# Sliding-window attention gated by a SwiGLU block: prologue, output stores, and weight casts tied to the last exponential

## The chip, the cores and the metric

The kernel runs on one core of a Trainium2 chip. A core has a tensor engine (PE, with its weight loads shown apart as PEld), a vector engine (DVE), a scalar engine (ACT), GpSimd (POOL) and a sync engine (SP), which here issues nearly all DMAs. Each engine works through its own list of instructions in order and waits on semaphores. The metric is the device time of one execution in microseconds (us); lower is better.

## The reference

The input x has 2048 tokens of 512 features. It is normalised once (layer norm without weights), and two branches read the result:

```
xn = layernorm(x)
q, k, v = split(xn @ wqkv)                 # 32 heads of 16
p = softmax(mask(q k^T / 4))               # each token sees itself and the 255 before it
s = (p v) @ wo                             # 512 -> 512
g = silu( (silu(xn @ w1) * (xn @ w3)) @ w2 )   # 512 -> 1792 -> 512
out = x + s * g
```

All inputs and the output are float32.

## The kernel before, in words

**Precision.** PE multiplies float16. A float32 operand is scaled by a power of two and cut into a high part (its float16 cast) and a low part (the rest, again float16); three products stand for one. The scale of a weight block comes from the sum of its squares. So each weight block has a path of its own: a load, squares (L249 on ACT or L251 on DVE for w1, w3 and the projections, L923 on ACT for w2), a cast of the sums (L261), a small matmul that adds them over the partitions (L285 when it stands beside scores), a chain of small DVE operations (L294 to L304, then L886 and L887, or L935 to L945 for w2), and the cut. `split_pool` makes the cut of most blocks: ACT scales (L342) and casts (L343), POOL subtracts in four pieces (L345). `split` does the same with ACT (L333) and DVE (L334).

**Tiles.** Tokens go in four tiles of 512 (t = 0 to 3). The hidden width of 1792 is 14 blocks f of 128. For each tile and block, `gate_up` makes 24 matmuls of 128x512 (L1036) into two PSUM banks; ACT takes a tanh (L1051) from one, DVE multiplies (L1055, L1060). `down` (L1261) multiplies by w2 in four groups of blocks: 0 to 3, 4 to 7, 8 to 10 and 11 to 13. In tile 0 the weights are prepared and stored to device memory; later tiles load them ready made. Tiles 2 and 3 use a folded product with w2 (L1179).

**Attention.** 32 units of four heads each (t, g, p): four head groups g and two pairs p in a tile. `pass1` makes scores (L665) and DVE takes their maxima (L679); a later pass, `pass2`, makes scores again transposed (L746), DVE adds the mask (L753), ACT takes the exponential (L756), and PE multiplies by the values (L774). `project` makes keys and queries (L597), whose banks ACT (L614) and DVE (L618) empty; they go to device memory and `fetch` (L641) brings them back in another layout. `total` multiplies by wo (L1313), joins the branches and stores the output (L1324).

**PSUM.** Two single banks `m0` and `m1` are taken in turn by `bank()`; two pairs of banks `s` hold scores (`scores_bank()`); one pair `po` holds the result of attention and some scores.

**What sets the order.** The Python program traces instructions one after another. PE's order is exactly the traced one. On the other engines a scheduler sets the order at build time: among instructions that are ready in its own model of time it takes those traced first, with a priority for what is traced inside `urgent()` (exponentials, tanh, and what empties banks among them). It can therefore put an instruction ahead of others that were traced before it. `tc.issue_after(ins)` forbids that for one instruction: what is traced in it comes behind `ins` on `ins`'s engine. `behind_exp()` is this with the last exponential traced so far; before the change it was used for the squares of w2 (L923) and a few more.

**Steps.** Time in the program is counted in steps: one after each batch of attention rows and after each piece of dense work (six matmuls, mostly). `later(n, f)` runs f when n more steps have passed. `beside_scores(n, f)` puts f, after n steps, at the head of the list from which a batch of `pass1` takes its next side work. `measure(f, apart)` does the squares of blocks f and f + 1 (both w1 and w3), `apart` steps from each other, then the scale beside scores after 8 steps, then the four cuts: 1, 2, 4 and 6 steps behind the scale for f below 8, else 1, 5, 9 and 13. `measure_down(k, f)` does it for group k of w2, with the cuts 1, 3, 5 and 7 steps behind.

**The prologue** (L1505 to L1596) loads x and the first weights while PE runs filler matmuls (`keep_busy`, L1537). It normalises and transposes tile 0 and projects head groups 0 and 1, with `fetch` one step behind each. The scores of the first unit begin at the first L665.

SBUF for weights and streams is a list of 54 slots, `take` and `give`; a slot that is given back can name a number of steps before it is taken again.

Of the kernel before, what the change touches and what calls it, by code (L numbers as in the profile page):

```python
# [10 lines left out]
F32 = mybir.dt.float32  # L11
# [10 lines left out]
P = 128  # L22
S = 2048
D = 512
# [59 lines left out]
def tile_block(ctx: ExitStack, tc: tile.TileContext, x, wqkv, wo, w1, w3, w2, out):  # L84
# [155 lines left out]
    def squares(parts, on_act=0, apart=0):  # L240


        ssq = small.tile([P, len(parts)], F32, name="ssq")

        def one(i, raw):

            sq = ppool.tile([P, D], BF16, name="sqa" if i < on_act else "junk", bufs=1)
            if i < on_act:
                nc.scalar.activation(sq, raw, AF.Square, accum_out=ssq[:, i:i + 1])  # L249
# [12 lines left out]
        def behind_bank():  # L262

            with tc.issue_after(lasts["emptied"].ins) if "emptied" in lasts else nullcontext():
                cast()
        if apart:
            later(apart * (len(parts) + 1) + 1, behind_bank)
        else:
            cast()
        return sb  # L270
# [310 lines left out]
    def project(t, g, k, terms=(range(3),), scores_bank=False):  # L581
# [7 lines left out]
        def part(n):  # L589
# [1 line left out]
            w = WQ[t, g, k]  # L591
            xh, xl = X[t]
            if n == 0:
                cell["pp"] = pss.tile([P, 2, TW], F32, name="s")[:, 0, :] if scores_bank else bank([P, TW])
            for c, i in parts[n]:
                a, b = ((0, xh), (1, xh), (0, xl))[i]
                nc.tensor.matmul(cell["pp"], w[:, (a * NC + c) * P:(a * NC + c + 1) * P], b[:, c, :], start=(c, i) == parts[0][0],  # L597
# [33 lines left out]
        WQ[t, g, k] = w = take(F16)  # L631
        nc.sync.dma_start(w, dWQ[g, k])

    def fetch(t, g):
        QA[t, g] = qa = qpool.tile([P, 4, TW], F16, name="qa")
        ka = keys(t, g)
        c0 = 0 if t else 2 * P
        for dst, d in ((ka[:, :, c0:], dK[g][:, :, t * TW - 2 * P + c0:(t + 1) * TW]),
                       (qa, dQ[g][:, :, t * TW:(t + 1) * TW])):
            for r in range(2):  # L640
                lasts["load"] = nc.sync.dma_start(dst[64 * r:64 * r + KR],  # L641
                                  d[64 * r:64 * r + 64].rearrange("(a d) i t -> (d i) a t", d=DH))

# [224 lines left out]

    measured = set()

    def measure(f, apart=0):

        raws = [RAW.pop(f + i) for i in range(2)]
        sb = squares([raws[0][0], raws[1][0], raws[0][1], raws[1][1]], on_act=4 if f > 2 else 2, apart=apart)
# [7 lines left out]
        def rest(pp, pi):  # L884
            ff = slice(f, f + 2)
            nc.vector.tensor_scalar(sg_scale[:, ff], pp[:, 0, :], 0.5 / (WS * XS), None, op0=ALU.mult)  # L886
            nc.vector.tensor_mul(p13[:, ff], pp[:, 0, :], pp[:, 1, :])  # L887
            measured.update((f, f + 1))

            def cut(i, k):  # L890
                if k == 0:
                    WF[0, f + i] = [[None, None], WF.pop((0, f + i), [None, None])[1]]
                WF[0, f + i][0][k] = a = take(F16)
                split_pool(a[:, 0:D], a[:, D:], raws[i][k], pi[:, k, i:i + 1])
                give(raws[i][k], after=5)
            for i in range(2):
                for k in range(2):
                    later(((1, 2, 4, 6) if f < 8 else (1, 5, 9, 13))[2 * i + k], lambda i=i, k=k: cut(i, k))
        if started:
            beside_scores(8, scale)  # L900
        else:
            later(10 if apart else 6, scale)

# [11 lines left out]
    def measure_down(k, f):  # L915
# [17 lines left out]
        def rest(p2):  # L933
# [13 lines left out]
            def cut(f):  # L947
                raw = RAW2.pop(f)
                WF.setdefault((0, f), [[None, None], None])[1] = b = take(F16)
                if k == 0:  # L950
                    with tc.issue_after(lasts["emptied"].ins):
                        split(b[:, 0:D], b[:, D:], raw, sw[:, f - f0:f - f0 + 1])
                else:
                    split_pool(b[:, 0:D], b[:, D:], raw, sw[:, f - f0:f - f0 + 1])
                give(raw, after=5)
            for i, f in enumerate(range(f0, f1)):
                later(1 + 2 * i, lambda f=f: cut(f))
# [335 lines left out]
    def total(t, b):  # L1293
# [4 lines left out]
        def part(half):  # L1298
# [16 lines left out]
            if half:  # L1315
# [10 lines left out]
                if t == NT - 1:  # L1326
                    store()
                else:
                    later(4, store)
                if b == 3:  # L1330
                    give(*(OT[t, g] for g in range(NG)))
        return opening([(6, lambda h=h: part(h)) for h in range(2)])
# [22 lines left out]
    def feed_forward():  # L1355
# [4 lines left out]
        for t in range(NT):  # L1360
            for f in range(FB):
                if t == 0:
# [3 lines left out]
                    elif f + LEAD == FB - 1:  # L1366
                        pieces += [(0, lambda f=f: load(0, f)) for f in range(FB - 2, FB)]
                    if f % 2 and f + 3 < FB:
                        pieces.append((0, lambda f=f + 3: later(5, lambda: measure(f, 1)) if f == 6 else measure(f, 1)))
# [161 lines left out]
        nc.gpsimd.memset(KA[2][:, a, :].bitcast(F32), TWO_ONES)  # L1531


    def keep_busy(n):
        ps = bank([P, 4, P])
        for _ in range(n):
            nc.tensor.matmul(ps, onesb, onesb.unsqueeze(1).to_broadcast([P, 4, P]), start=True, stop=True)  # L1537

# [19 lines left out]
        flush()  # L1558
    with tc.issue_after(lasts["hi"].ins), tc.issue_after(lasts["x"].ins):
        qk[1][1]()  # L1560
    keep_busy(4)


    k00, q00 = (project(0, 0, k, ((0,), (1,), (2,)), k) for k in (1, 0))
    run([k00[0], q00[0], k00[1]])
    qk[1][2]()
    with tc.issue_after(lasts["scale"].ins):
# [2 lines left out]
    qk[1][3]()  # L1570
    with tc.issue_after(lasts["hi"].ins):
        run([k00[2], q00[2]])
    later(1, lambda: fetch(0, 0))
    k01 = project(0, 1, 1, ((0, 2), (1,)))
    run(k01[:1])
    wv[2]()
# [4 lines left out]
    sc["o"] = scaled(SQ["wv"][3], OS / WS, "so")  # L1581
    with tc.issue_after(lasts["hi"].ins):
        measure(0)
    run(project(0, 1, 0, scores_bank=True))
    later(1, lambda: fetch(0, 1))
    run(value(0, True))
    qk[2][1]()
# [89 lines left out]
```

## Time and profile before

| | |
|---|---|
| runs, median (lowest to highest) | 811.51 us (811.1 to 811.94), 3 runs |
| the profiled execution | 811.24 us |
| its span, from the first to the last instruction | 809.4 us |
| PE busy | 793.7 us of the span |
| DVE busy | 631.2 us |
| ACT busy | 392.1 us |
| POOL busy | 377.1 us |
| granted clock of PE | 1.00 in all stretches |

All durations below come from the profiled execution, whose own time is 811.24 us. A row of the timeline gives the start and the duration in us, the engine, the line, the operation, what it writes and reads, the count of instructions that the row joins, and in brackets the idle time of that engine before it and what ended it. A row of the waits gives who waited for whom, the sum, the times and the longest. A row of the stretches gives the stretch, its length, the busy time of PE, PEld, DVE, ACT and POOL with their counts, the granted clock, the busy share of the DMA engines and GB/s. An "SPq" row is a DMA issue on SP's queue, not the transfer.

### The profile page before, as it was taken

The numbers are of one execution on the slowest core, as the hardware profiler recorded it, in microseconds if no ns is written. First come the engines' busy times: TensorE is split into PE (matmuls) and PEld (weight loads), VectorE is DVE, ScalarE is ACT, GpSimd is POOL, SyncE is SP. The second block draws the span as 40 slices with busy tenths as digits, with TensorE's granted clock in tenths as the row PEclk, the third lists the DMA queues.
The fourth block names the chain that finished last, engine by engine and source line by source line (L and its number), as shares of the span: only waits on it lengthen the run. The fifth ranks groups of instructions, "written<-read, shape, count | busy, mean of one in ns | idle before, by whom it ended". The sixth has DMA issues, their size and how long they took to land.

```text
span 809.4 us, 23944 instructions
## 1 busy us (share of the span) xinstructions
PE 793.7 (98%) x9176; PEld 403.7 (50%) x9176; DVE 631.2 (78%) x2037; ACT 392.1 (48%) x591; POOL 377.1 (47%) x732
## 2 busy tenths in 40 slices
PE   8999989999999999999999999999999999999998
PEld 4444444444444444444444454456544754466465
DVE  8788788887888777887988888777778787875437
ACT  6879586553546544345344433344444234344411
POOL 2345376342329445354353455530346276550670
PEclk9999999999999999999999999999999999999999
DMA  9968554835576474757655634646372644335321
GB/s 282 265 214 267 160 183 134 278 114 191 160 199 208 134 232 139 218 142 263 160 162 181 194 104 119 185 137 179 105 201 74 160 139 137 113 90 172 111 65 62
DMA packets 109795, 134.19 MB, mean 166 GB/s; under 512 B 18864, under 2 KB 64880, under 8 KB 109680
## 3 DMA queue, kind: packets, MB, share of 16 engines
q1 hardware_dynamic: 109392, 132.13, 54.6%
q8 instruction: 72, 1.18, 0.6%
q10 hardware_dynamic: 288, 0.52, 0.2%
q14 instruction: 43, 0.35, 0.1%
HBM read 91.23 MB, written 36.57 MB: 158 GB/s over the span
## 4 chain that ended last, share of the span: by engine, by line
PE 79%; DVE 8%; ACT 6%; DMA 3%; issue 2%; SPq 1%; POOL 0%; ACTq 0%; DVEq 0%
PE m L1036 30%; PE po L774 8%; PE m L1261 8%; PE m L1179 8%; PE m L597 7%; PE s L746 5%; PE m L1313 4%; PE m L567 4%; PE s L665 3%; DMA slot<-in_B_w_dram 2%; DVE junk L679 2%; PE po L665 2%; ACT slot L342 1%; ACT pt L756 1%; ACT sqa L249 1%
## 5 line engine op out<-in xcount | busy, mean ns | idle before, releaser
L1036 PE MATMUL m<-XH,slot 128*128 128x512 f16 x896 | 267.4, 380 | 1.6 <-DVE slot L618 1.2
L756 ACT ACTIVATE pt<-s,es 128x1024 f32<-128x1024 f32 x152 | 167.5, 1112 | 193.7 <-DVE s L753 186.5
L1036 PEld LDWEIGHTS <-slot 128*128 128x128 f16 x1344 | 124.7, 98 | 156.0 <-issue 12.0
L1036 PE MATMUL m<-XL,slot 128*128 128x512 f16 x448 | 169.9, 379 | 0.0
L753 DVE TENSOR_TENSOR s<-s,MK 128x256 f32<-128x256 f32 (+2 forms) x280 | 118.7, 434 | 51.2 <-PE s L746 47.0
L679 DVE CUSTOM_DVE_ANT_0 junk<-s,MW 128x320 bf16<-128x320 f32 x276 | 133.9, 485 | 17.9 <-PE s L665 10.3
L339 POOL TENSOR_TENSOR slot<-slot,slot 128x256 f16<-128x256 f32 (+1 forms) x86 | 57.7, 692 | 141.9 <-ACT slot L1069 76.7
L345 POOL TENSOR_TENSOR slot<-slot,slot 128x128 f16<-128x128 f32 x168 | 69.1, 446 | 58.3 <-ACT slot L343 58.3
L679 DVE CUSTOM_DVE_ANT_0 junk<-po,MW 128x320 bf16<-128x320 f32 x172 | 83.4, 485 | 4.7 <-DVE mt L704 0.3
L1261 PE MATMUL m<-slot,slot 128*128 128x512 f16 x336 | 78.6, 380 | 0.3 <-DVE slot L1055 0.3
L774 PE MATMUL po<-pt,V 64*32 64x320 f32 (+4 forms) x2880 | 77.2, 342 | 0.8 <-DVE pp L304 0.8
L597 PE MATMUL m<-XH,slot 128*128 128x512 f16 x240 | 71.0, 380 | 1.6 <-DVE slot L1055 1.2
L1179 PE MATMUL m<-slot,slot 128*128 128x256 f16 x588 | 68.4, 273 | 0.0
L1094 POOL TENSOR_TENSOR slot<-slot,slot 128x256 f16<-128x256 f32 x98 | 64.6, 671 | 1.1
L1051 ACT ACTIVATE slot<-m,sgs 128x512 f32<-128x512 f32 x56 | 38.3, 683 | 54.4 <-PE m L1036 52.3
L774 PEld LDWEIGHTS po<-pt,V 64*32 64x32 f32 x2880 | 50.5, 106 | 22.9 <-PE s L515 0.9
L1179 PEld LDWEIGHTS <-slot 128*128 128x128 f16 x588 | 56.1, 98 | 11.5 <-issue 3.0
L1055 DVE SCALAR_TENSOR_TENSOR slot<-slot,m 128x512 f32<-128x512 f32 x56 | 38.3, 684 | 29.0 <-ACT slot L1051 29.0
L746 PE MATMUL s<-qa,KA 50*64 50x320 f16 (+3 forms) x1472 | 58.4, 260 | 0.1
L597 PEld LDWEIGHTS <-slot 128*128 128x128 f16 x384 | 35.6, 98 | 44.8 <-issue 3.4
L746 PEld LDWEIGHTS <-KA 50*64 50x64 f16 x1472 | 30.1, 106 | 51.9 <-issue 30.9
L1261 PEld LDWEIGHTS <-slot 128*128 128x128 f16 x336 | 30.7, 98 | 38.6 <-issue 4.2
(189 smaller groups left out, 1138.5 us busy)
## 6 DMA issues: line engine op xcount, KB each, us to landing
slot<-dW SPq DMA_DIRECT2D x98, 256.0 KB
slot<-in_B_w_dram SPq DMA_DIRECT2D x56, 256.0 KB
slot<-dFold SPq DMA_DIRECT2D x48, 256.0 KB
dW<-slot SPq DMA_DIRECT2D x42, 256.0 KB
slot<-in_A_x_dram SPq DMA_DIRECT2D x30, 256.0 KB
KA<-dK SPq DMA_DIRECT2D x24, 288.0 KB
qa<-dQ SPq DMA_DIRECT2D x32, 192.0 KB
slot<-dWQ SPq DMA_DIRECT2D x24, 256.0 KB
```

The lines of the kernel that those rows point to most:

```text
L339: op(out[:, c], a[:, c], b[:, c])
L345: nc.gpsimd.tensor_sub(lo[:, c:c + P], raw[:, c:c + P], hi[:, c:c + P])
L597: nc.tensor.matmul(cell["pp"], w[:, (a * NC + c) * P:(a * NC + c + 1) * P], b[:, c, :], start=(c, i) == parts[0][0], stop=(c, i) == parts[ ...
L679: lasts["maximum"] = nc.vector.tensor_tensor_reduce(out=junk[:, :n], in0=s[:, r, :n], in1=mask, scale=1.0, scalar=NEG, op0=ALU.add, op1=AL ...
L746: nc.tensor.matmul(s[64 * h:64 * h + 64, r, o:o + 64 * n], ka[rows, 2 * p + a, 64 * (m + 4):64 * (m + 5)], qa[rows, 2 * p + a, 64 * (m + k ...
L753: nc.vector.tensor_add(v, v, MK[:, kind, of:of + n, :].unsqueeze(1).to_broadcast([P, 2 * len(which), n, 64]))
L756: lasts["exp"] = nc.scalar.activation(pt, s, AF.Exp, scale=es)
L774: nc.tensor.matmul(cell["po"][32 * i:32 * i + 32, h, 64 * (m + k):64 * (m + k + n)], V[64 * h:64 * h + 64, (4 * t + m // 2) % VB, hd * VW: ...
L1036: nc.tensor.matmul(cell[k], w[:, (a * NC + c) * P:(a * NC + c + 1) * P], b[:, c, :], start=c == 0 and i == 0, stop=c == NC - 1 and i == 2)
L1094: nc.gpsimd.tensor_sub(lo, view, hi)
L1179: nc.tensor.matmul(cell["ps"][:, c], made[:, f:f + P], wj[:, g:g + 256], start=j == j0 and c == 0 and n == 0, stop=j == j1 - 1 and n == 2, ...
L1261: nc.tensor.matmul(ps, hh[:, a * TW + b * P:a * TW + (b + 1) * P], w[:, c * D:(c + 1) * D], start=f == f0 and i == 0, stop=f == f1 - 1 and ...
```

## The change

Six edits:

- **Filler.** The last call of `keep_busy` in the prologue makes three matmuls instead of four, and writes them into the scores bank that the first projection of keys then takes, not into an `m` bank.
- **First fetch.** `fetch(0, 0)` reads keys and queries in two pairs of heads, eight DMAs instead of four; the first unit needs the first pair alone.
- **Measuring of blocks 6 and 7.** It begins 8 steps behind its piece instead of 5, and its scale goes in 6 steps later instead of 8.
- **Ties.** The cuts of blocks 8 to 13 of w1 and w3, and those of w2's second to fourth group, are traced inside `behind_exp()`. Of `split_pool` this binds the two ACT instructions; POOL's follow by their data.
- **Output stores.** For tiles 0 to 2 the store of `total` is traced 10 steps behind it instead of 4.
- **Squares set apart.** Their cast is traced `apart * len(parts) + 2` steps on instead of `apart * (len(parts) + 1) + 1`.

```diff
@@ squares
-            later(apart * (len(parts) + 1) + 1, behind_bank)
+            later(apart * len(parts) + 2, behind_bank)
@@ project
-                cell["pp"] = pss.tile([P, 2, TW], F32, name="s")[:, 0, :] if scores_bank else bank([P, TW])
+                cell["pp"] = bank([P, TW]) if scores_bank is False else scores_bank()[:, 0, :]
@@ fetch
-    def fetch(t, g):
+    def fetch(t, g, ps=None):
...
-        for dst, d in ((ka[:, :, c0:], dK[g][:, :, t * TW - 2 * P + c0:(t + 1) * TW]),
-                       (qa, dQ[g][:, :, t * TW:(t + 1) * TW])):
-            for r in range(2):
-                lasts["load"] = nc.sync.dma_start(dst[64 * r:64 * r + KR],
-                                  d[64 * r:64 * r + 64].rearrange("(a d) i t -> (d i) a t", d=DH))
+        for heads in (slice(0, 4),) if ps is None else [slice(2 * p, 2 * p + 2) for p in ps]:
+            for dst, d in ((ka[:, heads, c0:], dK[g][:, :, t * TW - 2 * P + c0:(t + 1) * TW]),
+                           (qa[:, heads, :], dQ[g][:, :, t * TW:(t + 1) * TW])):
+                for r in range(2):
+                    rows = slice(64 * r + DH * heads.start, 64 * r + DH * heads.stop)
+                    lasts["load"] = nc.sync.dma_start(dst[64 * r:64 * r + KR],
+                                      d[rows].rearrange("(a d) i t -> (d i) a t", d=DH))
@@ measure
-    def measure(f, apart=0):
+    def measure(f, apart=0, until=8):
...
+            def tied(i, k):
+                with behind_exp():
+                    cut(i, k)
             for i in range(2):
                 for k in range(2):
-                    later(((1, 2, 4, 6) if f < 8 else (1, 5, 9, 13))[2 * i + k], lambda i=i, k=k: cut(i, k))
+                    if f < 8:
+                        later((1, 2, 4, 6)[2 * i + k], lambda i=i, k=k: cut(i, k))
+                    else:
+                        later((1, 5, 9, 13)[2 * i + k], lambda i=i, k=k: tied(i, k))
         if started:
-            beside_scores(8, scale)
+            beside_scores(until, scale)
@@ measure_down, cut
-                    split_pool(b[:, 0:D], b[:, D:], raw, sw[:, f - f0:f - f0 + 1])
+                    with behind_exp():
+                        split_pool(b[:, 0:D], b[:, D:], raw, sw[:, f - f0:f - f0 + 1])
@@ total
-                    later(4, store)
+                    later(10, store)
@@ feed_forward
-  later(5, lambda: measure(f, 1)) if f == 6 else measure(f, 1)
+  later(8, lambda: measure(f, 1, 6)) if f == 6 else measure(f, 1)
@@ prologue
-    def keep_busy(n):
-        ps = bank([P, 4, P])
+    def keep_busy(n, ps=None):
+        ps = bank([P, 4, P]) if ps is None else ps
...
-    keep_busy(4)
+    waiting = scores_bank()
+    keep_busy(3, waiting[:, 0, :].rearrange("p (k q) -> p k q", q=P))
...
-    k00, q00 = (project(0, 0, k, ((0,), (1,), (2,)), k) for k in (1, 0))
+    k00, q00 = (project(0, 0, k, ((0,), (1,), (2,)), (lambda: waiting) if k else False) for k in (1, 0))
...
-    later(1, lambda: fetch(0, 0))
+    later(1, lambda: fetch(0, 0, (0, 1)))
...
-    run(project(0, 1, 0, scores_bank=True))
+    run(project(0, 1, 0, scores_bank=scores_bank))
```

More of the change, by code (lines that the diff above doesn't have):

```diff
@@ L1368, in feed_forward @@
                     if f % 2 and f + 3 < FB:
-                        pieces.append((0, lambda f=f + 3: later(5, lambda: measure(f, 1)) if f == 6 else measure(f, 1)))
+                        pieces.append((0, lambda f=f + 3: later(8, lambda: measure(f, 1, 6)) if f == 6 else measure(f, 1)))
                     pieces += [(0, lambda f=f: load_down(0, f)) for f in range(f + 2 if f else 0, min(f + 3, FB))]
```

## The prediction

> **What bounds the kernel now.** I read the page first, then the waits of PE, then the busy time by stretches, and then the timeline around each wait.
>
> ```profile
> span 809.4 us, 23944 instructions
> PE 793.7 (98%) x9176; PEld 403.7 (50%) x9176; DVE 631.2 (78%) x2037; ACT 392.1 (48%) x591; POOL 377.1 (47%) x732
> ```
>
> TensorE (PE) is busy for 793.7 of 809.4 us, and its order is the program's own. The change removes one of its 9176 matmuls. So all that can be won by it is idle time of PE: 809.4 - 793.7 = 15.7 us. The stretches (length, then PE, PEld, DVE, ACT and POOL busy) say where that lies:
>
> ```profile
> 60.00:80.00 20.00, 18.70 (x147) 8.24 (x146) 17.10 (x64) 18.92 (x37) 10.86 (x22) 1.00 0.83 267
> ...
> 119.00:136.00 17.00, 15.54 (x233) 8.12 (x223) 15.45 (x57) 13.56 (x26) 9.83 (x24) 1.00 0.41 124
> 136.00:160.00 24.00, 24.00 (x289) 11.87 (x288) 18.82 (x67) 12.07 (x22) 10.66 (x24) 1.00 0.75 250
> 160.00:172.00 12.00, 10.81 (x97) 4.72 (x95) 10.24 (x41) 10.37 (x17) 8.79 (x22) 1.00 0.31 106
> 172.00:809.40 637.40, 632.78 (x7676) 328.33 (x7668) 490.25 (x1505) 264.30 (x349) 294.33 (x521) 1.00 0.51 152
> ```
>
> Behind 172 us PE idles 637.40 - 632.78 = 4.62 us in all, the end of the kernel included; ahead of it 15.7 - 4.6 = 11.1 us. In the stage ahead of 172 us weights are measured, cast and projected beside the first attention units, and in 60 to 80 us ScalarE (ACT) is busy for 18.92 of 20. What ends PE's waits (in total, times, longest):
>
> ```profile
> PE s L665 <- ACT pt L756: 2.4, 2, 1.6
> PE m L1036 <- DVE slot L618: 1.2, 2, 1.0
> PE m L597 <- DVE slot L1055: 1.2, 1, 1.2
> ...
> PE po L665 <- DVE M L679: 0.8, 1, 0.8
> ...
> PE po L665 <- DVE XL L525: 0.6, 1, 0.6
> PE m L1537 <- DVE XL L501: 0.6, 1, 0.6
> ...
> PE m L597 <- DVE slot L618: 0.5, 1, 0.5
> PE s L665 <- DMA qa<-dQ: 0.4, 1, 0.4
> ...
> PE m L1261 <- DVE slot L1055: 0.3, 1, 0.3
> ```
>
> Nearly all are waits for a PSUM bank that ACT or VectorE (DVE) has not yet emptied. They are short and many; the change can win several small terms and no large one.
>
> **The change part by part.** First the prologue.
>
> ```profile
> 12.85 1.02 PE L1537 MATMUL m<-onesb 128*128 128x512 bf16 x4 [0.58 <-DVE XL L501]
> 13.71 1.03 PE L597 MATMUL s<-XH,slot 128*128 128x512 f16 x4
> ...
> 30.15 0.30 PE L665 MATMUL s<-KA,qa 48*64 48x128 f16 x7 [0.41 <-DMA qa<-dQ]
> ```
>
> The four filler matmuls wait 0.58 us for the bank that DVE still reads, and the first projection (13.71) stands directly behind them. After the change there are three, in the scores bank that this projection uses anyway, so their wait goes, and one matmul of (13.71 - 12.85) / 4 = 0.22 us with it: at most 0.8 us. What is late next is the last XH copy and DVE's chain of casts, which nobody moves, so the bounds are 0 and 0.8, and I take half, 0.4.
>
> The first fetch is cut into pairs of heads, so that the first unit waits for half the bytes.
>
> ```profile
> 24.48 0.82 SPq L641 DMA_DIRECT2D KA<-dK  x2
> 25.39 0.88 SPq L641 DMA_DIRECT2D qa<-dQ  x2
> ```
>
> Four issues cost 0.82 + 0.88 = 1.7 us of SyncE's queue (SP); eight would cost 3.4. The four that the first unit needs are the first four, so the wait of 0.41 us at 30.15 should go: I take 0.4. The other end is a loss of 1.7 us, if what is queued behind on SP (the stores of the next group's keys and queries, weight loads, the second fetch) is awaited; no PE wait but this one ends on a DMA in the list above, so I stay at the row. The prologue gives 0.8.
>
> Second, the measuring of blocks 6 and 7, three steps later (8 instead of 5), its scale one step later in all (8 + 6 against 5 + 8).
>
> ```profile
> 70.43 0.64 ACT L249 ACTIVATE sqa<-slot 128x512 bf16<-128x512 f32 x1
> ...
> 71.06 0.72 ACT L333 ACTIVATE slot<-slot,sw 128x512 f16<-128x512 f32 x1
> ...
> 72.18 0.69 ACT L1051 ACTIVATE slot<-m,sgs 128x512 f32<-128x512 f32 x1
> 72.76 0.63 ACT L249 ACTIVATE sqa<-slot 128x512 bf16<-128x512 f32 x1
> ```
> ```profile
> 71.81 0.89 DVE L334 SCALAR_TENSOR_TENSOR slot<-slot,sw,slot 128x512 f16<-128x512 f32 x1 [0.71 <-ACT slot L333]
> ...
> 72.96 0.67 DVE L1055 SCALAR_TENSOR_TENSOR slot<-slot,m 128x512 f32<-128x512 f32 x1
> ```
> ```profile
> 87.99 1.11 ACT L756 ACTIVATE pt<-s,es 128x1024 f32<-128x1024 f32 x1 [8.03 <-DVE s L753]
> ```
>
> The squares at 70.43 and 72.76 (L249) are two of the four of block 6's measuring. ACT runs without a pause there, and DVE idles 0.71 us for the cast (L333) that stands behind the first of them; the bank that PE awaits is then freed at 72.96 + 0.67. Without the square at 70.43 that cast comes 0.63 us earlier (71.06 - 70.43), and DVE with it. The waits that hang on this chain are the 0.3 us of L1261 on L1055 and the 0.8 on L679; I take 1.0 of these 1.1, nearest to what the DVE row shows, between 0 and 1.1. The squares go where ACT stands idle for 8.03 us. By the steps in the code the scale is put in 14 instead of 13 steps after the piece that starts it, and the batch that takes it up is the 17th, so the casts of blocks 6 and 7 hardly move.
>
> Third, the ties. A cast (L342, L343 on ACT, then four subtractions L345 on POOL) of blocks 8 to 13 was traced 1, 5, 9 and 13 steps behind its scale, but ACT takes them nearly in one run, ahead of exponentials traced earlier:
>
> ```profile
> 164.27 1.34 ACT L342 ACTIVATE slot<-slot,pi 128x512 f32<-128x512 f32 x2
> 165.51 0.61 ACT L343 CAST slot<-slot 128x512 f16<-128x512 f32 x1
> 166.02 1.11 ACT L756 ACTIVATE pt<-s,es 128x1024 f32<-128x1024 f32 x1
> ```
> ```profile
> 165.05 0.29 DVE L753 TENSOR_TENSOR s<-s,MK 128x128 f32<-128x128 f32 x1
> ```
>
> The mask of that exponential is ready at 165.05 + 0.29 = 165.34, and it starts at 166.02: 0.7 us are the casts'. PE waits for exponentials 2.4 us in two places, 1.6 and so 0.8; this is the 0.8. With the ties two of these casts go behind it. I take 0.7 of the 0.8 + 0.5 us of PE waits in 160 to 172 us, between 0 and 1.2.
>
> ```profile
> 107.53 1.32 ACT L342 ACTIVATE slot<-slot,pi 128x512 f32<-128x512 f32 x2
> ...
> 114.44 1.33 ACT L342 ACTIVATE slot<-slot,sw 128x512 f32<-128x512 f32 x2 [1.23 <-DVE sw L945]
> ...
> 117.33 1.09 ACT L756 ACTIVATE pt<-s,es 128x1024 f32<-128x1024 f32 x1
> ```
> ```profile
> 106.77 6.98 POOL L345 TENSOR_TENSOR slot<-slot,slot 128x128 f16<-128x128 f32 x16
> ```
> ```profile
> 111.66 0.39 DVE L304 TENSOR_SCALAR pp<-al 128x4 f32<-128x4 f32 x1
> ...
> 113.68 0.72 DVE L945 TENSOR_SCALAR sw<-p,q 128x4 f32<-128x4 f32 x1
> 114.32 0.68 DVE L1055 SCALAR_TENSOR_TENSOR slot<-slot,m 128x512 f32<-128x512 f32 x1
> ```
> ```profile
> L304 DVE TENSOR_SCALAR pp<-al x11: 159/163/714, 30.1 to 203.5; 128x4 f32<-128x4 f32 x9, 128x3 f32<-128x3 f32 x2
> ```
>
> Around 115 us PE waits 1.2 us for L1055, which DVE's chain up to L945 holds up, and then 1.6 us for the exponential at 117.33. The two casts of w2 at 114.44 hold that exponential up, but they were traced behind the exponential before it, so the tie leaves them in front. What the tie does here is to move three of the four casts of blocks 8 and 9 (107.53 is the second pair) from ahead of 110 us into 111 to 127, and their twelve subtractions with them. That clears POOL while DVE's chain runs: L304 took 0.39 us under POOL's run of sixteen, its median is 163 ns, so 0.23 us were lost, and L945's 0.72 holds a like loss. I take 0.6 of the 2.8 us; the bounds are a gain of 2.8 and the loss of the rivals below.
>
> The Trainium skill, page "SBUF — State Buffer", section "SBUF: two separate sides", says that DVE operations of certain kinds and POOL operations take turns on one pair of ports, whole instructions at a time; the row of L304 agrees. It speaks against the change as much as for it: subtractions that leave one chain of DVE meet another.
>
> The casts of blocks 10 and 11 that are moved back, and those of w2's third group, fall into 136 to 160 us, where PE is busy for 24.00 of 24.00; those of w2's last group fall behind 172 us. There the feed-forward matmuls hide them: nothing to win, and one cast in front of an exponential, 1.3 us (worked out below), to lose if that cover is gone. Output stores ten instead of four steps later take waits out of SP's queue behind 172 us, where no PE wait ends on a DMA: nothing, and if the two slots that each store holds six steps longer ran short, a load would be late by as much. The new count of steps for a cast of squares is the old one for blocks (4 + 2 against 5 + 1) and one less for wo (8 + 2 against 10 + 1), behind 172 us too: nothing.
>
> **Sum.** 0.8 + 1.0 + 0.7 + 0.6 = 3.1 us. The profiled execution took 811.24 us (span 809.4), so 808.1; the median of the runs, 811.51, lies 0.27 higher, so I say 808.4.
>
> **The rivals.** *Slower: the moved casts fill ACT where it has no room.* One cast is 1.34 / 2 + 0.61 = 1.3 us of ACT. Three land in 111 to 127 us, where the only pause quoted is 1.23 us (114.44), and two more behind 166 us. If each ends up in front of an exponential or a tanh, 5 x 1.3 - 1.2 = 5.3 us are handed to PE. The gains of the first two parts, 1.8, stay: at full price 811.5 - 1.8 + 5.3 = 815.0, and it decides from 1.8 us on, that is from two such casts; at two thirds, 3.5, the time is 813.2. Against it: the next exponential's mask is ready only a batch later, and exponentials have priority. Chance 0.13.
>
> *The subtractions meet DVE elsewhere.* DVE is busy for 15.45 of 17 us in 119 to 136. Twelve subtractions that each stretch an operation by 0.23 us cost 2.8, so that the 0.6 turns into a loss of some 2.2: 811.5 - 2.5 + 2.2 = 811.2. The Trainium skill's section on the port pair, named above, is the rule behind it. Chance 0.12.
>
> *Given back.* PE's longest wait for L618, 1.0 us, stands in the timeline behind the prologue, and it is for a bank that ACT empties first; if ACT's queue there is not shifted with PE, the prologue's 0.8 us are lost: 809.2. Chance 0.15.
>
> *The ties do nothing*, because the order of ACT comes out the same: 811.5 - 1.8 = 809.7. Chance 0.10.
>
> *Both waits around 115 us go:* 2.2 us more, 806.2. Chance 0.10. The forecast itself has 0.40.
>
> **How the numbers follow.** A measurement of this kernel can tell about 0.2% from no change, 1.6 us: faster means below 809.9, slower above 813.1. The forecast (0.40), the better case (0.10), most of "given back" and half of "ties do nothing" are faster: 0.64. Half of the slower rival and a little of the ports lie above 813.1: 0.11. The rest, 0.25, is the same. The range goes from 805.5, somewhat below the better case, to 813.2, the slower rival at two thirds.
>
> **What would show it.** The filler matmuls without an idle time before them, and the first L665 without a wait for qa; L249 gone from 70 to 73 us, found after 75, and no wait for M L679 near 76 us; L342 of block 12 in the timeline behind the exponential near 166 us; POOL's run of sixteen L345 broken up, and L304 at its median. PE busy time must stay near 793.5. It would be wrong if ACT's exponentials behind 110 us start later after their masks than now, if PE's waits for ACT rise above 2.4 us, or if idle PE time appears behind 172 us, where I see none to win.

## The result, and the profile after

The changed kernel takes 808.81 us (median of 8 runs, 808.41 to 811.14), the kernel before 811.24 beside it (8 runs, 811.1 to 812.24): a ratio of 0.9971, 95% interval 0.9962 to 0.998. The forecast was 808.4. By the medians 2.4 us are won, where 3.1 were forecast. The profiled execution took 808.41 us and is the fastest of its eight, so the 2.8 us between the two profiles are somewhat more than the typical gain. Its page, after:

```profile
span 806.6 us, 23981 instructions
...
PE 793.0 (98%) x9175; PEld 403.8 (50%) x9175; DVE 630.3 (78%) x2037; ACT 392.6 (49%) x591; POOL 377.9 (47%) x732
```

PE's work is what it was (793.7 before); the span is 2.8 us shorter, so PE's idle time has fallen from 15.7 to 13.6 us and its busy time by 0.7, the filler matmul among it. PE's waits, after (who waited for whom, sum, times, longest):

```profile
PE po L776 <- DVE pp L304: 1.5, 1, 1.5
PE s L667 <- ACT pt L758: 1.1, 3, 0.7
...
PE m L1045 <- DVE slot L618: 0.8, 2, 0.6
PE m L597 <- DVE slot L1064: 0.7, 1, 0.7
PE po L667 <- DVE M L681: 0.7, 1, 0.7
...
PE m L597 <- DVE slot L618: 0.6, 1, 0.6
```

Lines are shifted by the diff: L776 here is L774 before, L667 is L665, L758 is L756, L1045 is L1036, L1064 is L1055, L681 is L679. The wait for exponentials fell from 2.4 to 1.1, that for L618 from 1.2 to 0.8 and that for L1064 from 1.2 to 0.7. The wait of 0.4 for qa is gone. The first line is new in this size: 1.5 where before had 0.8.

**The lead.** PE works through the same list in both kernels, fillers aside, so the n-th matmul of one stands against the n-th of the other, and the difference of their starts is the lead there. The first projection shows how (before, 13.71):

```profile
12.04 0.81 PE L1546 MATMUL s<-onesb 128*128 128x512 bf16 x3
13.01 1.02 PE L597 MATMUL s<-XH,slot 128*128 128x512 f16 x4 [0.16 <-ACT XH L496]
```

The three fillers no longer wait, and 13.71 - 13.01 = 0.70 us. Taken in this way at places of the kernel before (us), the lead over it is:

| kernel | 17 | 55 | 82 | 119 | 130 | 171 | 250 | 420 | 620 | 805 |
|---|---|---|---|---|---|---|---|---|---|---|
| changed | 0.5 | 1.8 | 1.9 | 3.2 | 2.6 | 2.9 | 3.2 | 3.1 | 3.1 | 3.1 |
| filler and fetch | 0.6 | 1.9 | 1.9 | 1.9 | 1.9 | 2.0 | 1.5 | 0.7 | 0.7 | 0.7 |
| ties | 0 | -0.1 | 0 | 1.3 | 0.7 | 1.0 | 0.9 | 0.8 | 0.8 | 0.6 |
| measuring | -0.1 | -0.1 | 0 | 0.1 | 0.1 | 0.1 | 0.1 | 0 | -0.4 | -0.4 |
| stores, squares' cast | -0.1 | -0.1 | -0.1 | -0.1 | -0.1 | -0.1 | 0.1 | 0.1 | 0.1 | 0.1 |
| filler, fetch, stores | 0.2 | 1.5 | 1.6 | 1.6 | 1.6 | 1.6 | 1.1 | 1.1 | 0.1 | 0.1 |
| filler, fetch, stores, squares' cast | 0.4 | 1.7 | 1.7 | 1.7 | 1.7 | 1.7 | 1.7 | 1.7 | 1.6 | 1.5 |
| all but measuring | 0.5 | 1.7 | 1.8 | 3.1 | 2.5 | 2.8 | 3.0 | 3.0 | 3.0 | 3.0 |

The lower rows are the experiments below. Ahead of 10 us executions differ by some 0.3 us in a wait that no edit touches, so rows are compared by how they go on. Each row is one execution. The end gives 0.27 us back: from the last store's issue to the end of the span are 3.69 us before and 3.95 after,

```profile
805.73 1.43 SPq L1352 DMA_DIRECT2D out_dram<-slot  x2
```
```profile
802.67 1.43 SPq L1361 DMA_DIRECT2D out_dram<-slot  x2
```

(before, then after). So does every run that has the divided fetch in it; why was not tried.

### The profile page after: what moved, and what is told of

Its sections match the earlier page's. It is cut to its first block, busy times and chain, and to the rows that moved or that the text cites. A ratio compares the mean times of both kernels' runs of the same rounds, so it can differ in the third digit from the quotient of the medians.

```text
span 806.6 us, 23981 instructions
## 1 busy us (share of the span) xinstructions
PE 793.0 (98%) x9175; PEld 403.8 (50%) x9175; DVE 630.3 (78%) x2037; ACT 392.6 (49%) x591; POOL 377.9 (47%) x732
## 4 chain that ended last, share of the span: by engine, by line
PE 81%; ACT 6%; DVE 5%; DMA 3%; issue 2%; SPq 2%; POOL 0%; DVEq 0%; ACTq 0%
PE m L1045 29%; PE m L1270 9%; PE po L776 9%; PE m L597 8%; PE m L1188 8%; PE s L748 5%; PE m L567 4%; PE m L1322 4%; PE s L667 3%; PE po L667 2%; ACT pt L758 1%; DMA slot<-in_B_w_dram 1%; ACT slot L342 1%; DMA slot<-in_A_x_dram 1%; DVE junk L681 1%
## 5 line engine op out<-in xcount | busy, mean ns | idle before, releaser
L1045 PE MATMUL m<-XH,slot 128*128 128x512 f16 x896 | 267.3, 380 | 1.2 <-DVE slot L618 0.8
L758 ACT ACTIVATE pt<-s,es 128x1024 f32<-128x1024 f32 x152 | 167.7, 1113 | 192.0 <-DVE s L755 188.5
L1045 PEld LDWEIGHTS <-slot 128*128 128x128 f16 x1344 | 125.0, 98 | 155.1 <-issue 11.7
L1045 PE MATMUL m<-XL,slot 128*128 128x512 f16 x448 | 169.8, 379 | 0.0
L681 DVE CUSTOM_DVE_ANT_0 junk<-s,MW 128x320 bf16<-128x320 f32 x276 | 134.1, 486 | 17.5 <-PE s L667 9.8
L339 POOL TENSOR_TENSOR slot<-slot,slot 128x256 f16<-128x256 f32 (+1 forms) x86 | 57.6, 693 | 123.0 <-ACT slot L1078 50.6
L681 DVE CUSTOM_DVE_ANT_0 junk<-po,MW 128x320 bf16<-128x320 f32 x172 | 83.5, 485 | 4.7 <-DVE al L298 0.5
L776 PE MATMUL po<-pt,V 64*32 64x320 f32 (+4 forms) x2880 | 77.2, 342 | 1.5 <-DVE pp L304 1.5
L1060 ACT ACTIVATE slot<-m,sgs 128x512 f32<-128x512 f32 x56 | 38.3, 684 | 55.1 <-PE m L1045 54.8
L776 PEld LDWEIGHTS po<-pt,V 64*32 64x32 f32 x2880 | 50.5, 106 | 23.6 <-issue 2.4
L1064 DVE SCALAR_TENSOR_TENSOR slot<-slot,m 128x512 f32<-128x512 f32 x56 | 38.4, 685 | 29.5 <-ACT slot L1060 29.3
```

Source lines behind the costliest of these rows:

```text
L339: op(out[:, c], a[:, c], b[:, c])
L681: lasts["maximum"] = nc.vector.tensor_tensor_reduce(out=junk[:, :n], in0=s[:, r, :n], in1=mask, scale=1.0, scalar=NEG, op0=ALU.add, op1=AL ...
L758: lasts["exp"] = nc.scalar.activation(pt, s, AF.Exp, scale=es)
L776: nc.tensor.matmul(cell["po"][32 * i:32 * i + 32, h, 64 * (m + k):64 * (m + k + n)], V[64 * h:64 * h + 64, (4 * t + m // 2) % VB, hd * VW: ...
L1045: nc.tensor.matmul(cell[k], w[:, (a * NC + c) * P:(a * NC + c + 1) * P], b[:, c, :], start=c == 0 and i == 0, stop=c == NC - 1 and i == 2)
```

## Experiments: the parts alone

Each part was put into the kernel before by itself. Theory A is read off the lead of the changed kernel, theory B is the sum of the prediction.

**Filler and fetch alone.**

```diff
-    keep_busy(4)
+    waiting = scores_bank()
+    keep_busy(3, waiting[:, 0, :].rearrange("p (k q) -> p k q", q=P))
...
-    later(1, lambda: fetch(0, 0))
+    later(1, lambda: fetch(0, 0, (0, 1)))
```

> Filler and first fetch alone, everything else as before. Theory A, read off the trace of the changed kernel (PE reaches the same matmuls 1.8 us earlier at 55 us, and no later edit has acted by then): 1.8 us less than the kernel before, still 1.8 at the end. Theory B, the sum on record: 0.8 us less. Theory C, 'given back': less at 50 us, nothing left at the end.

810.79 us, ratio 0.9994 (0.9985 to 1.0003). Up to 171 us theory A holds: 1.95 us of lead, more than twice the 0.8 of the prediction. Behind 171 us theory C holds: two new waits take 1.25 of it. The waits of PE behind 172 us, in this run:

```profile
PE m L597 <- DMA slot<-dWQ: 0.6, 1, 0.6
PE s L285 <- DVE sb L261: 0.5, 1, 0.5
```

Neither is in the kernel before. The first is a load that came late. SP's queue in this run, around it:

```profile
325.77 0.91 SPq L1014 DMA_DIRECT2D dFold<-slot  x2
333.87 0.34 SPq L1326 DMA_DIRECT2D out_dram<-slot  x1
334.25 0.43 SPq L632 DMA_DIRECT2D slot<-dWQ  x1
```

and what SP waited for there (sum, times, longest):

```profile
SPq L1326 <- POOL slot L339: 7.1, 1, 7.1
```

SP stands for 7.1 us at the output store, whose addition POOL has not finished, and the load of dWQ (L632) is queued behind it, though it needs nothing of it. In the kernel before SP stands there as well (4.4 and 1.4 us), but issues the load at 332.97, and PE starts on it at 338.11 without a wait; here PE is there at 336.80 and waits until 337.40. In the changed kernel the same queue reads:

```profile
324.38 0.48 SPq L632 DMA_DIRECT2D slot<-dWQ  x1
324.95 1.24 SPq L1021 DMA_DIRECT2D dFold<-slot  x1
332.21 0.34 SPq L1333 DMA_DIRECT2D out_dram<-slot  x1
```

There the store is traced six steps later, and the load goes out 7.8 us ahead of it (332.21 - 324.38).

**Ties alone.**

```diff
+                        later((1, 5, 9, 13)[2 * i + k], lambda i=i, k=k: tied(i, k))
...
+                    with behind_exp():
+                        split_pool(b[:, 0:D], b[:, D:], raw, sw[:, f - f0:f - f0 + 1])
```

> The ties alone (w1, w3 and w2). Theory A: about 1.2 us less: 1.3 won at 113 to 119 us, 0.7 lost near 130 us in the wait of L774's bank, 0.4 won at 164 to 171. Theory B, the sum on record: 1.3 us less, 0.6 of it around 115 us and 0.7 at 160 to 172, nothing lost at 130. Theory C: the ties need the earlier prologue or the later measuring to act, and alone they give under 0.5.

810.63 us, ratio 0.999 (0.9981 to 0.9998). Theory A place by place: 1.3 won by 119 us, 0.66 lost at 130, 0.35 won by 171. C falls: the ties act by themselves. But 0.4 of the 1.0 us is lost behind 171 here, which A did not foresee: 0.15 near 237 us, where PE waits 0.20 us for the same sb as in the run before, the rest near 717 us.

**Measuring alone.**

```diff
+  later(8, lambda: measure(f, 1, 6)) if f == 6 else measure(f, 1)
```

> The later measuring of blocks 6 and 7 alone. Theory A: 0.1 us less, since two squares still stand in ACT's queue between 71 and 73 us and the 0.8 us wait of L665 on L679 near 76 us stays. Theory B, the sum on record: 1.0 us less.

811.42 us, ratio 1.0 (0.9991 to 1.0009): nothing, theory A. ACT's and DVE's rows of this run show why:

```profile
70.50 0.73 ACT L333 ACTIVATE slot<-slot,sw 128x512 f16<-128x512 f32 x1
71.12 0.63 ACT L923 ACTIVATE sqa<-slot 128x512 bf16<-128x512 f32 x1
...
72.24 0.69 ACT L1051 ACTIVATE slot<-m,sgs 128x512 f32<-128x512 f32 x1
```
```profile
72.97 0.69 DVE L1055 SCALAR_TENSOR_TENSOR slot<-slot,m 128x512 f32<-128x512 f32 x1 [0.61 <-ACT slot L1051]
```

The cast (L333) that stood behind a square is free of it and starts at 70.50 instead of 71.06. But a square of w2 (L923) takes the place of the square that left. So the tanh (L1051) starts at 72.24 (72.18 before), and DVE's multiplication L1055, which idles 0.61 us for that tanh, at 72.97 (72.96 before). The squares that were moved don't reach ACT's long pause either: they start at 73.43, and the pause that ends at 87.99 is still 7.82 us (8.03 before). PE's waits between 73 and 77 us add up to 1.12 us (0.21, 0.28 and 0.63), in the kernel before to 1.10 (0.26 and 0.84).

**Output stores and squares' cast alone.**

```diff
-                    later(4, store)
+                    later(10, store)
...
-            later(apart * (len(parts) + 1) + 1, behind_bank)
+            later(apart * len(parts) + 2, behind_bank)
```

> The later output stores and the squares' cast alone. Both theories: nothing, within 0.3 us, the traces alike up to 172 us. A rival by which the small gain behind 172 us (0.15 us from 171 to 806 us) is the stores': 0.2 us less.

811.26 us, ratio 0.9999 (0.999 to 1.0008): nothing that these runs can tell from zero. The lead does grow by 0.23 us between 171 and 250 us, as the rival has it. Still the sum of the parts alone, 0.7 + 0.6 - 0.4 + 0.1 = 1.0 us of lead at the end, is a third of the 3.06 that they give together. By the medians it is 0.5 + 0.7 - 0.1 + 0.0 = 1.1 of 2.4 us.

## Experiments: what keeps the lead

**Filler, fetch and stores.** The first run's edits and `later(10, store)`.

> Filler, first fetch and the later output stores; no ties, no later measuring, the squares' cast as before. The run with the prologue alone led by 1.95 us up to 171 us, then lost 0.48 at 236 us (PE's wait for sb, L261) and 0.78 around 337 us, where SP's queue stood 7 us at an output store and the load of dWQ behind it came 0.6 us late. Theory A (the later stores cover the second loss): no wait for dWQ near 337 us, the loss at 236 us stays, about 1.45 us less than before, 809.85. Theory B (the stores do nothing for it): 0.6 us less, as with the prologue alone.

810.38 us, ratio 0.9988 (0.998 to 0.9997). The wait for dWQ is gone, the one for sb stays, as theory A says. But a third one comes that it did not name, at 528 us, and takes 0.9: PE waits for L1057 (L1055 before), and DVE is late there because its reciprocal (L823) stands 3.8 us for a DMA. This third wait may be this execution's own: at 811.38 us it is one of the two slowest of eleven (median 810.38), and the run with the measuring alone, which has none of these edits, loses 0.4 us at the same place.

**The squares' cast with them.** The same and `later(apart * len(parts) + 2, behind_bank)`.

> The same with the squares' cast one step earlier for wo. Theory A: the wait for sb near 236 us goes too, and all of the 1.95 us is left at the end: 809.35. Theory B: the wait at 236 us stays or moves, and the time is that of the run before it.

809.82 us, ratio 0.9982 (0.9973 to 0.9991), 1.5 us under the kernel before: the wait at 236 us is gone, the one at 528 too, and of 1.7 us of lead at 171 1.5 are left. So the two edits that are worth nothing alone hold 0.8 us here that the prologue would lose. That the wait at 528 us went with it was not expected. If it comes and goes between executions, as the run with the measuring alone suggests, no edit took it away; more executions were not profiled.

**The filler alone** (one execution, 811.87 us).

> The filler alone: how much of the lead of 1.9 us at 55 us is the filler's. Theory A: 0.6 at 16 us, and it grows by the smaller wait for L618 at 54 us (1.03 to 0.62) with the filler alone, since it moves PE's matmuls in the two m banks by one: 1.2 or more at 56 us, and the wait of 0.4 us for qa at 30 us stays or grows. Theory B: 0.6 at 16 us is all, or it is lost at 30 us in a longer wait for qa, 0.2 or less left at 56 us; the rest is the fetch's.

The lead is 0.5 at 17 us, -0.1 at 31, 0.6 at 55 and 0.45 at 82. The waits of PE up to 56 us:

```profile
PE s L665 <- DMA qa<-dQ: 1.0, 2, 0.6
PE m L1036 <- DVE p2qk L304: 0.9, 1, 0.9
```

Without the divided fetch PE comes 0.5 us earlier to a transfer that is no earlier, and waits 1.0 instead of 0.4. Of the 1.9 us some 0.45 are the filler's alone, and the fetch adds 1.5 on top. Both theories are partly right: the lead is lost at 30 us, and 0.7 comes back between 42 and 55, in four steps at 42.3, 45.3, 51.6 and 55.3 us. With filler and fetch these four places give 1.0 (0.2, 0.2, 0.15 and 0.4). Only the last of them, the wait for L618, stands in the list of waits; what the first three are the traces don't show. At 528 us this run loses 1.0 as well. DVE there, and in the kernel before:

```profile
525.13 0.35 DVE L821 RECIPROCAL dr<-dr 128x32 f32<-128x32 f32 x1 [3.85 <-DMA dr<-os]
```
```profile
524.34 0.35 DVE L821 RECIPROCAL dr<-dr 128x32 f32<-128x32 f32 x1 [2.61 <-DMA dr<-os]
```

PE is 0.45 us earlier, the reciprocal 0.8 later. The DMA that it awaits is issued at 517.32 instead of 517.08, behind the loads in SP's queue; the other 0.55 us of the delay come between that issue and the reciprocal. The mask, the exponential and the tanh stand behind the reciprocal.

**All but the measuring.** The changed kernel with `later(5, lambda: measure(f, 1))` as before.

> The changed kernel without the later measuring of blocks 6 and 7; all else as changed. Theory A (the squares at 71 to 73 us end none of PE's waits): 2.9 us ahead of before at 171 us as the changed kernel is, and the same time, 808.8. Theory B, the sum on record: the measuring is worth 1.0 us, so 809.8, and PE waits more between 71 and 77 us than in the changed kernel. Theory C: up to 171 us as A, but something later is given back, as in the runs with the prologue alone: 809.3 to 810.

808.58 us, ratio 0.9963 (0.995 to 0.9975): theory A. The lead is 2.8 at 171 us and 3.0 at the end, the changed kernel's 2.9 and 3.1. The measuring is worth 0.1 at most, alone or with the rest.

## Experiments: the wait that the ties made

In the changed kernel four engines show the place:

```profile
121.69 0.73 ACT L342 ACTIVATE slot<-slot,pi 128x512 f32<-128x512 f32 x1
122.31 0.69 ACT L1060 ACTIVATE slot<-m,sgs 128x512 f32<-128x512 f32 x1
```
```profile
123.58 3.12 POOL L345 TENSOR_TENSOR slot<-slot,slot 128x128 f16<-128x128 f32 x8
```
```profile
126.28 0.45 DVE L298 TENSOR_SCALAR al<-al 128x4 int32<-128x4 int32 x1
```
```profile
127.80 0.96 PE L776 MATMUL po<-pt,V 64*32 64x320 f32 x28 [1.49 <-DVE pp L304]
```

A tied cast (L342) stands right ahead of a tanh (L1060). Before, the tanh started at 125.18, and the lead at that place is 3.23, so 121.95 was to be expected; 122.31 is 0.36 late. DVE's multiplication L1064 then idles 0.71 us for the tanh instead of 0.34, and behind it DVE has hardly a pause up to L304. Then L298 takes 0.45 us under POOL's run of eight instead of 0.16. 0.36 + 0.29 = 0.65, the growth of the wait from 0.82 to 1.49. The 0.29 is tried below; the 0.36 is read from these rows alone, and no run takes it away.

**The last cut of block 9 later.**

```diff
-                        later((1, 5, 9, 13)[2 * i + k], lambda i=i, k=k: tied(i, k))
+                        later((1, 5, 9, 17 if f == 8 else 13)[2 * i + k], lambda i=i, k=k: tied(i, k))
```

> The changed kernel with the last cut of block 9 traced 17 instead of 13 steps behind its scale, so that its ACT part stands behind the next exponential. In the changed kernel PE's wait for L776's bank near 128 us is 1.5 us instead of 0.8. Theory A: of the 0.67 us more, 0.37 is the cast (L342) that holds up the tanh L1060, and 0.29 is L298 stretched by POOL's subtractions of the same cut; both go, the wait falls back to 0.8 and the time to 808.15. Theory B: the wait has another cause (the longer DVE chain behind L525, say) and stays at 1.5; the time stays 808.8.

808.54 us, ratio 0.996 (0.9947 to 0.9972). Neither theory in full: PE loses 0.38 us at this place instead of 0.66. L298 is back at 0.16, but the tanh is as late as it was, with another instruction where the cast stood:

```profile
121.77 0.62 ACT L931 ACTIVATE sqa<-slot 128x512 bf16<-128x512 f32 x1
...
122.39 0.68 ACT L1060 ACTIVATE slot<-m,sgs 128x512 f32<-128x512 f32 x1
```
```profile
127.59 2.04 PE L776 MATMUL po<-pt,V 64*32 64x320 f32 x72 [1.02 <-DVE XL L525]
```

The place in front of the tanh is filled by whatever is ready; in the kernel before a square (L249) stood there. The row of PE also shows what the bank waits for. The other profiles name L304, but here L304 starts at 127.65, later than PE; it is L525, the last to read the bank, that lets PE go. L298 counts because it stands ahead of L525 in DVE's order. The gain is gone again by 250 us (lead 3.1, like the changed kernel).

**The subtractions later, the casts where they are.** Of two cuts POOL's part is put behind POOL's next addition; the orders of ACT and DVE stay.

```diff
+        def low():
+            with tc.issue_after(lasts["halves"].ins) if n else nullcontext():
+             for c in range(0, 512, P): nc.gpsimd.tensor_sub(lo[:, c:c + P], raw[:, c:c + P], hi[:, c:c + P])
+        later(n, low) if n else low()
...
+                split_pool(a[:, 0:D], a[:, D:], raws[i][k], pi[:, k, i:i + 1], 8 if (f, i, k) == (8, 1, 1) else 0)
...
+                        split_pool(b[:, 0:D], b[:, D:], raw, sw[:, f - f0:f - f0 + 1], 8 if f == 7 else 0)
```

> The changed kernel with the POOL subtractions of the last cut of block 9 and of block 7 of w2 put behind POOL's next addition (L339), ACT's and DVE's orders untouched: POOL is then clear while DVE works off L294 to L304 before PE's wait for L776's bank. Theory A, the two share something as the row of L298 says (0.45 us under POOL's run of eight, 0.16 without): L298 takes 0.16 us and the wait falls from 1.5 to 1.2 us, 808.5. Theory B: L298 is stretched by something else; nothing changes, 808.8.

808.53 us, ratio 0.9965 (0.9951 to 0.9979). Theory A to the hundredth:

```profile
126.24 0.16 DVE L298 TENSOR_SCALAR al<-al 128x4 int32<-128x4 int32 x1
```
```profile
127.47 2.04 PE L777 MATMUL po<-pt,V 64*32 64x320 f32 x72 [1.20 <-DVE pp L304]
129.44 1.77 PE L1271 MATMUL m<-slot,slot 128*128 128x512 f16 x6
```

The wait falls from 1.49 to 1.20. But the next row takes 1.77 us for six matmuls that took 1.47 in the changed kernel: they read block 7 of w2, whose low part is now late, and the 0.3 us are lost again at once.

**Only block 9's subtractions later.** The same for one cut, with the one for which PE waited left in place.

> The changed kernel with only the subtractions of block 9's last cut behind POOL's next addition; those of block 7 of w2, for which PE waited in the run with both moved (its lead over the changed kernel fell from 0.34 us at 130 us to 0.03 at 134), stay where they are. Theory A: L298 takes 0.16 us again, PE's wait for L776's bank is 1.2 us, and nothing is given back behind it: 0.3 us ahead of the changed kernel from 130 us to the end, 808.1 to 808.5. Theory B: POOL's run of four that is left still meets the chain, or PE waits for block 9 in its turn: no lead left at 171 us.

808.49 us, ratio 0.9965 (0.9951 to 0.9978). L298 takes 0.16, the wait is 1.21, and the lead over the changed kernel is 0.29 us from 130 to 171 us. Of the rows of PE the second shows the six matmuls back at 1.47, and the third where the 0.29 go:

```profile
127.51 2.04 PE L777 MATMUL po<-pt,V 64*32 64x320 f32 x72 [1.21 <-DVE pp L304]
129.49 1.47 PE L1271 MATMUL m<-slot,slot 128*128 128x512 f16 x6
...
235.05 0.59 PE L1046 MATMUL m<-XH,slot 128*128 128x512 f16 x2 [0.21 <-DVE slot L1295]
```

In the changed kernel the last of these starts at 235.03 without a wait. DVE sets the time. The row for 220 to 235 us in this run (busy: PE, PEld, DVE, ACT, POOL):

```profile
220.00:235.00 15.00, 14.84 (x172) 7.18 (x171) 14.24 (x47) 4.54 (x5) 3.36 (x6) 1.00 0.53 132
```

DVE is busy for 14.24 of 15 us with squares of wo (L251) beside the attention's work. That the same matmul starts at 235.03 and 235.05 speaks for a limit of some 3.1 us on the lead there, past which idle time saved ahead of it does not show (the leads of the last four runs at 250 us are 3.0 to 3.2); a kernel with less of DVE's work there was not tried.

**The squares tied as well.** The changed kernel, and L249 tied like the casts.

```diff
+                with behind_exp() if apart else nullcontext(): nc.scalar.activation(sq, raw, AF.Square, accum_out=ssq[:, i:i + 1])
```

> The changed kernel with the squares that are set apart (L249 on ACT) tied behind the last exponential too, as its casts are. Theory A: exponentials and tanhs held up by squares are what is left of ACT's part, so L249 leaves 71 to 73 us, PE's waits of 0.7 us for L681 near 74 us and for the exponential near 115 us fall below 0.3, and the wait of 1.5 us for L776's bank near 127 us falls by the 0.4 us that a cast holds up a tanh: 1.0 to 1.5 us less than the changed kernel, 807.3 to 807.8. Theory B: the scales come later with the squares, the weights' casts crowd in behind them, and PE waits for the cut blocks: 808.8 or more.

812.72 us, ratio 1.0008 (0.9997 to 1.0019). That is theory B in its direction, but most of it goes with PE's clock (last section): eleven of the twelve runs have a mean clock of 0.995 to 0.998 and took 810.37 to 814.22 us; the one at 1.0 took 809.19, 0.4 above the changed kernel. The waits of PE in the profiled execution (812.38 us):

```profile
PE po L776 <- DVE pp L304: 3.0, 1, 3.0
PE s L285 <- DVE sb L261: 1.9, 1, 1.9
PE po L667 <- DVE M L681: 1.3, 1, 1.3
...
PE s L285 <- DVE sb L935: 0.9, 1, 0.9
```

ACT's urgent work is on time: the longest wait for an exponential is 0.2 instead of 0.7 us, and the waits for L1064 and L618 near 112 and 162 us are gone. But PE adds the squares over the partitions itself (L285), at a fixed place of its order, and what it adds is not there: 1.9 + 0.9. The wait of 3.0 us is a DVE operation under POOL's subtractions again:

```profile
128.22 2.04 DVE L298 TENSOR_SCALAR al<-al 128x4 int32<-128x4 int32 x1
```
```profile
125.57 4.67 POOL L345 TENSOR_TENSOR slot<-slot,slot 128x128 f16<-128x128 f32 x12
```

The subtractions stand in one run of twelve here, and L298 ends with that run (125.57 + 4.67 = 130.24): 2.04 us instead of 0.16. No other operation of these chains takes half as long in the traces of this case, and the execution of 809.19 us leaves no room for all of these waits; how often it happens is not shown. The wait for L681 near 75 us grew to 1.3 although the squares had left the front of that exponential: they were not its cause.

## Why the prediction was right, and by which of its steps

The time was right, the sum behind it was not: 1.9 + 0.1 + 0.35 + 0.65 stands for 0.8 + 1.0 + 0.7 + 0.6. That both come to about 3 is luck: the first term was 1.1 too small, the second 0.9 too large, and the first is kept to the end only by two edits that were priced at nothing.

| step | forecast | shown | by |
|---|---|---|---|
| filler and fetch | 0.8 | 1.9 up to 171 us | filler and fetch alone |
| measuring | 1.0 | 0.1 at most | measuring alone; all but measuring |
| ties at 160 to 172 us | 0.7 | 0.35 | ties alone |
| ties around 115 us | 0.6 | 1.3, and 0.65 lost at 130 us | ties alone |
| stores, squares' cast | 0 | 0 alone, 0.8 with the prologue | the parts in turn |

**Filler and fetch.** The two steps were right (fillers without a wait, no wait for qa), the term too small. Besides 0.6 at the fillers and 0.35 at the wait for qa, PE gains 1.0 between 42 and 55 us, for which the sum had nothing. The wait for L618 near 54 us, by which the rival "given back" was to eat the gain, shrank instead, from 1.03 to 0.64.

**Measuring.** The step that failed is "Without the square at 70.43 that cast comes 0.63 us earlier (71.06 - 70.43), and DVE with it". The cast came 0.56 us earlier alone, but L1055 waits for the tanh, and in front of the tanh another square took the place. In the kernel before, with the measuring alone, in the changed kernel and with the squares tied, 3.9 to 4.0 us pass from the start of this multiplication to the end of the maximum (L679, L681) that frees the bank, and DVE stands still for some 0.15 of them. So "the waits that hang on this chain" hang on the tanh and on DVE's own row, not on that cast, and with the squares tied they stayed although the squares had gone.

**Ties at 160 to 172 us.** As forecast, the cast of block 12 stands behind the exponential:

```profile
163.10 1.11 ACT L758 ACTIVATE pt<-s,es 128x1024 f32<-128x1024 f32 x1 [1.06 <-DVE s L755]
164.11 0.68 ACT L1060 ACTIVATE slot<-m,sgs 128x512 f32<-128x512 f32 x1
164.68 0.72 ACT L342 ACTIVATE slot<-slot,pi 128x512 f32<-128x512 f32 x1
```

PE's wait for it fell from 0.73 to 0.15; 0.2 of that was lost to L618 just ahead.

**Ties around 115 us.** Here the chosen 0.6 between 2.8 and a loss came out by two larger terms of opposite sign. POOL's and DVE's rows, after:

```profile
108.73 1.30 POOL L339 TENSOR_TENSOR slot<-slot,slot 128x256 f16<-128x256 f32 x2 [1.91 <-ACT slot L1078]
112.50 1.58 POOL L345 TENSOR_TENSOR slot<-slot,slot 128x128 f16<-128x128 f32 x4 [2.47 <-ACT slot L343]
```
```profile
111.60 0.23 DVE L953 TENSOR_SCALAR sw<-p,q 128x4 f32<-128x4 f32 x1
```

The run of sixteen is broken up, and POOL is clear from 110.03 to 112.50 us, while the end of DVE's chain runs: L953 (L945 before) takes 0.23 us instead of 0.72. Ahead of that L304 is back at 0.16, but L298 lost 0.24 under L339 in its stead. The exponential had less ahead of it: one of two casts (L343) and a square (L249) now stand behind it. Both waits fell to 0.73, so 1.3 were won. Of that 0.65 were lost at 130 us; that the rest meets the 0.6 is luck too. Both mechanisms of the slower rivals happened, once each with a price: a cast in front of a tanh (0.36) and a subtraction over a DVE operation (0.29). Their place was right, their count was not: one each instead of twelve stretches and several casts. The Trainium skill, page "SBUF — State Buffer", section "SBUF: two separate sides", gives the shared pair, between certain DVE operations and a POOL operation, to whoever starts first, for the whole instruction. The 0.29 us that L298 lost lie below the 3.12 / 8 = 0.39 us of one subtraction, and clearing POOL brought them back, so the runs agree with it. But one subtraction is not the most that an operation can lose: with the squares tied L298 lost 1.9 us, until the run of twelve was over.

**The zeros.** "Output stores ten instead of four steps later take waits out of SP's queue behind 172 us, where no PE wait ends on a DMA: nothing" is the step that failed in kind. It was true of the kernel before and is true of the edit alone. It isn't true of a kernel in which PE arrives 2 us earlier: SP's queue and DVE's chains don't all move with PE, and waits appear that were slack: 0.5 us for sb near 236 us and 0.6 for dWQ near 337 us, 1.25 of lead. The prediction named this as a sign of error (idle PE time behind 172 us) and did not see that two of the six edits were what kept it away.

## What to carry to other kernels

An engine that is busy for 98% of the time hides waits that are nearly there; time saved ahead of it is kept only if the queues beside it have that much slack, so look there for the transfer or the chain with the least, and price an edit that moves it together with the one that needs it. In a queue that issues in order, what waits for slow work belongs behind what somebody awaits soon. To move side work from in front of one urgent operation is to put it, or the next ready piece, in front of another; count where each lands.

## What the runs showed of the hardware

**PE's clock fell after short idle times.** The trace notes the granted clock by windows of 3.41 us. In the run with the squares tied, it halved (the column behind POOL) for one such window, behind PE's waits near 8 and 10 us:

```profile
7.13:10.54 3.41, 1.58 (x10) 0.60 (x9) 3.10 (x20) 1.90 (x5) 0.00 (x0) 1.00 1.11 338
10.54:13.96 3.42, 3.42 (x17) 3.22 (x17) 2.98 (x6) 1.79 (x4) 0.00 (x0) 0.50 1.14 300
13.96:17.37 3.41, 3.35 (x16) 1.27 (x14) 2.15 (x5) 3.31 (x9) 0.00 (x0) 1.00 1.14 292
```

At 17 us PE was 1.6 us behind the changed kernel. In the window ahead of the fall PE was busy for 1.58 us. The run with the last cut later has nearly the same waits, but its windows lie otherwise: in the one around them (7.56 to 10.98 us) PE was busy for 1.91 us, and the clock stayed at 1.00. It also stayed there in the run with the squares tied behind windows with 1.73 us (99.29 to 102.70) and 1.75 us (126.59 to 130.00). So in these traces the fall lies between 1.58 and 1.73 us of work in a window, and whether a wait reaches it depends on where the windows lie in that execution. The changed kernel's slowest run, 811.14 us, had a mean clock of 0.998. The Trainium skill, page "TensorE: Matmul & The Clock Gate", section "Part 1: The HAM clock gate (the "warmup" mystery)", has the clock halved after an idle window of about 3.4 us. The length agrees; but here PE was busy for 1.58 of the 3.41 us, so less idle time was enough.
